# Start-up queues, later loads and a residual by transfer in a fused cosine attention and low-rank mixer

## The chip, the core and the metric

The kernel runs on one core of a Trainium2 chip. The metric is the time of one execution on the device, in microseconds: 582.26 us before the change, the median of three runs (582.1 to 582.92). The profile is of one execution whose span, from the first to the last instruction, is 580.3 us. The engines are named as in the profile: PE multiplies matrices (PEld is its load of the stationary operand), DVE and ACT are the vector and scalar engines, POOL is GpSimd, and SP only issues transfers. SP, ACT and POOL each issue transfers in the order of their own program.

## The reference

Attention over 8 batches of 12 heads, 448 positions and 64 features, with normalised q and k, and then a mixer on the joined heads (768 channels):

```python
q_n = q / (np.linalg.norm(q, axis=-1, keepdims=True) + 1e-06)
k_n = k / (np.linalg.norm(k, axis=-1, keepdims=True) + 1e-06)
scores = np.matmul(q_n, k_n.transpose(0, 1, 3, 2)) / tau
attn = softmax(scores)
x = np.matmul(attn, v)                    # joined to (8, 448, 768)
u = x + (x.transpose(0, 2, 1) @ U @ V).transpose(0, 2, 1)   # rank 32
out = u + np.maximum(u @ w_ch1, 0.0) @ w_ch2                # 768 -> 3072 -> 768
```

The last line adds `u` itself, the residual, to the result of the two large products.

## The kernel before

Two heads make a pair. There are 48 pairs, numbered 0 to 47, six per batch, and the program goes through them in order. For each pair it transposes q and k (T), forms scores by key chunk (S), takes their exponential on ACT, multiplies by v (V), divides, and applies the low-rank product in three steps (A, then a transpose of the divided result X, then H), which leaves `u` transposed, in the tiles `uE` for even and `uO` for odd batches. The two large products of a batch, called M1 (`steps_m1`, L513) and M2 (`steps_m2`, L540), are cut into steps of six matmuls and put between the pairs of the following batch, as filling work for PE.

Inputs come in groups of pairs: groups 0 and 1 hold one pair each, all others two. So group 5 is pairs 8 and 9, group 6 pairs 10 and 11, group 7 pairs 12 and 13. `load` (L205 to L214) brings q, k or v of a group; q takes two transfers, k and v four. Class `Prep` then squares q and k, reduces, takes the root (ACT), inverts (DVE), scales (mostly POOL, L268) and copies v to bf16 (`values`, POOL, L276). Three staging buffers per input are used in turn.

Up to pair 6 the order of everything is written out by hand, in the string `ORDER`. Its words are: `sq0k.a` square k of group 0 on ACT, `red` reduce, `root`, `inv`, `sc` scale, `l3q` load q of group 3, `w62` issue 62 spare matmuls of the identity (L667), which do no work of the result but keep PE busy, `T0`, `Te0` transpose a pair and evict it, `S00` scores of pair 0, chunk 0, `ex00` its exponential, and so on. The identity `ident` is made by POOL and is needed by these spare matmuls and by the transposes of PE.

After that, `put(n, i, fn)` hangs a piece of work behind slot i of pair n, where pair NP is 6; `spread` runs the slots and shares M1 and M2 steps between them. The change and the reasoning touch these entries: the list `at` (squares of q and k, values, two reduces, root) and `when` (inverse and scales) of groups 5, 6 and 7, and the places of their loads. A class `Estimate` counts expected times and only decides which of ACT and DVE evicts a tile.

From pair 12 on, q and k (and X) are transposed by a transfer that SP issues (L315, L461) instead of by PE. For batches after the first, the residual is taken from `ut`: `turn` (L500) transposes half of `u` with one transfer, and DVE adds it as it evicts an M2 block (L558). For batch 0 the residual is instead added by three more matmuls with the identity at the end of each M2 block (L550), and ACT or DVE copies the block out (L554, L556). A half is 384 of the 768 output columns; an M2 block is 24 matmuls of 128x384. Each block is stored by two transfers on SP (L564, L568; for the last blocks of the last batch the second one is ACT's).

The weights `w1_sb` and `w2_sb` are loaded by eight transfers of POOL (L168, L173), from 20.9 us on. `load_mixer` (L137) clears some constants and loads U and V of the mixer on POOL's queue; `load_copies` (L159) loads three more copies of V, which `place_copies` spreads for the later pairs. `V_raw` and `ut` share a tag of two buffers.

## Time and profile before

| engine | busy us | share | instructions |
|---|---|---|---|
| PE | 568.6 | 98% | 5074 |
| DVE | 213.1 | 37% | 461 |
| ACT | 261.0 | 45% | 447 |
| POOL | 215.1 | 37% | 205 |

| group of PE instructions | count | busy us |
|---|---|---|
| L540, M2, 128x384 | 1344 | 233.6 |
| L513, M1, 128x448 | 1128 | 227.2 |
| L331, scores | 576 | 42.4 |
| L667, spare | 144 | 11.1 |
| L550, residual of batch 0 | 18 | 2.0 |

Times of a group are sums over its instructions, which overlap in PE's pipeline; the step from one start to the next is shorter than a mean duration. Six matmuls of M2 take 0.97 to 0.98 us in the chain of waits, so one takes 0.163 us, though the page gives it 327 ns. In the timeline a line gives the start, the length of a merged run, the engine, the line of the kernel and the operation, and in brackets how long the engine sat idle just before and what released it. The transfers moved 74.5 MB, 128 GB/s over the span and 223 to 240 GB/s from 30 to 80 us.

### The profile page before, as it was taken

To read this page: it belongs to the slowest core of one execution; us is meant where nothing else is said; L and a number is where in the kernel's file an instruction comes from. 1 tells how busy PE (TensorE), PEld (TensorE's weight loads), DVE (VectorE), ACT (ScalarE), POOL (GpSimd) and SP (SyncE) were. 2 spreads that over 40 slices of the span, in tenths; PEclk is the share of its full clock that TensorE was granted. 3 is DMA by queue.
4 is the path that set the end of the run, shared out by engine and by line. 5 is a ranking of instruction groups with operands and counts; after the bars stand their busy time and mean duration, and the time that the engine had idled before them with its cause. 6 is when DMAs were issued, how large, how long until landed. Compare 5 with 4: busy or idle time off the path is not lost.

```text
span 580.3 us, 12249 instructions
## 1 busy us (share of the span) xinstructions
PE 568.6 (98%) x5074; PEld 327.1 (56%) x5074; DVE 213.1 (37%) x461; ACT 261.0 (45%) x447; POOL 215.1 (37%) x205
## 2 busy tenths in 40 slices
PE   7999999999999999999999999999999999999997
PEld 6665565555565556555655555655555545655554
DVE  6874551433243334423324343432244332320011
ACT  5876544455333653446324455246443374214200
POOL 8754866515326236426055063253261420000000
PEclk9999999999999999999999999999999999999999
DMA  6999999767486375584465763783655640231022
GB/s 163 193 244 236 238 211 221 181 124 138 103 158 155 88 154 114 135 162 105 88 160 137 128 137 96 145 175 81 134 125 117 132 74 16 54 72 35 7 49 56
DMA packets 139673, 74.52 MB, mean 128 GB/s; under 512 B 86656, under 2 KB 139440, under 8 KB 139616
## 3 DMA queue, kind: packets, MB, share of 16 engines
q1 hardware_dynamic: 129344, 63.03, 50.0%
q0 software_dynamic: 9728, 10.18, 10.3%
q8 instruction: 40, 0.66, 0.4%
q10 hardware_dynamic: 544, 0.51, 0.3%
q14 instruction: 17, 0.14, 0.1%
HBM read 52.19 MB, written 11.01 MB: 109 GB/s over the span
## 4 chain that ended last, share of the span: by engine, by line
PE 87%; DMA 7%; DVE 2%; SPq 1%; ACT 1%; POOL 1%; issue 0%; DVEq 0%; POOLq 0%; ACTq 0%
PE mp L540 38%; PE mp L513 33%; DMA w_sb<-in_moe_w_ch_dram 5%; PE sc L331 5%; PE av L383 3%; PE up L383 2%; DMA kst<-in_k_dram 2%; PE av L343 1%; PE av L376 1%; PE up L376 1%; PE up L469 1%; DMA qst<-in_q_dram 1%; PE av L483 1%; DVE ss L248 1%; ACT E L356 0%
## 5 line engine op out<-in xcount | busy, mean ns | idle before, releaser
L540 PE MATMUL mp<-w_sb,relu 128*128 128x384 bf16 x1344 | 233.6, 327 | 0.8 <-DMA w_sb<-in_moe_w_ch_dram 0.8
L540 PEld LDWEIGHTS <-relu 128*128 128x128 bf16 x1344 | 125.2, 98 | 90.6 <-issue 14.0
L513 PEld LDWEIGHTS <-w_sb 128*128 128x128 bf16 x1128 | 105.0, 98 | 99.2 <-issue 9.3
L517 ACT ACTIVATE relu<-mp 128x448 bf16<-128x448 f32 x162 | 88.0, 543 | 128.4 <-PE mp L513 128.4
L356 ACT ACTIVATE E<-sc 128x896 bf16<-128x896 f32 x144 | 125.2, 923 | 23.6 <-PE sc L331 22.6
L268 POOL TENSOR_TENSOR qk<-kst,inv 128x512 bf16<-128x512 f32 x43 | 45.9, 1069 | 240.7 <-DVE inv L262 236.2
L513 PE MATMUL mp<-uO,w_sb 128*128 128x448 bf16 x576 | 114.3, 353 | 0.0
L513 PE MATMUL mp<-uE,w_sb 128*128 128x448 bf16 x552 | 112.9, 353 | 0.0
L558 DVE TENSOR_TENSOR o_sb<-mp,ut 128x384 f32<-128x384 f32 x50 | 27.8, 557 | 141.4 <-PE mp L540 140.1
L248 DVE TENSOR_REDUCE ss<-sq 128x16 f32<-128x1024 f32 (+1 forms) x50 | 57.8, 1165 | 1.0 <-ACT sq L240 1.0
L268 POOL TENSOR_TENSOR qk<-qst,inv 128x512 bf16<-128x512 f32 x44 | 47.3, 1077 | 1.6 <-PE up L441 1.6
L383 PEld LDWEIGHTS <-E 128*128 128x128 bf16 x1152 | 45.0, 97 | 0.0
L519 DVE TENSOR_SCALAR relu<-mp 128x448 bf16<-128x448 f32 x26 | 16.2, 625 | 78.0 <-PE mp L513 77.5
L331 PE MATMUL sc<-qkT 64*64 64x448 bf16 x576 | 42.4, 360 | 0.6 <-ACT E L356 0.3
L243 POOL TENSOR_TENSOR sq<-kst 128x1024 f32<-128x1024 f32 (+1 forms) x23 | 42.6, 1856 | 0.1
L243 POOL TENSOR_TENSOR sq<-qst 128x1024 f32<-128x1024 f32 x21 | 39.7, 1892 | 3.3 <-DMA qst<-in_q_dram 3.3
L353 ACT ACTIVATE E<-av 128x448 bf16<-128x448 f32 x17 | 9.2, 541 | 47.3 <-PE up L343 47.3
L276 POOL CAST v<-vst 128x1024 bf16<-128x1024 f32 (+1 forms) x25 | 25.0, 1003 | 9.9 <-DMA vst<-in_v_dram 7.7
L383 PE MATMUL av<-v,E 128*128 128x65 bf16 x624 | 28.0, 193 | 0.0
L473 ACT CAST A_sb<-up 128x128 bf16<-128x128 f32 x19 | 5.0, 263 | 47.6 <-PE up L469 47.6
L394 DVE RECIPROCAL rd<-av 128x4 f32<-128x4 f32 x52 | 9.3, 178 | 46.2 <-PE av L383 46.2
L376 PEld LDWEIGHTS <-E 128*128 128x128 bf16 x192 | 18.0, 98 | 14.6 <-issue 0.8
(98 smaller groups left out, 348.9 us busy)
## 6 DMA issues: line engine op xcount, KB each, us to landing
out_dram<-o_sb SPq DMA_DIRECT2D x109, 96.0 KB, 2.2
w_sb<-in_moe_w_ch_dram POOLq DMA_DIRECT2D x8, 1152.0 KB, 18.8
qst<-in_q_dram SPq DMA_DIRECT2D x23, 256.0 KB, 3.9
vst<-in_v_dram SPq DMA_DIRECT2D x46, 128.0 KB, 2.9
kst<-in_k_dram SPq DMA_DIRECT2D x44, 128.0 KB, 2.8
qst<-in_q_dram SPq DMA_DIRECT2D x23, 192.0 KB, 4.0
vst<-in_v_dram SPq DMA_DIRECT2D x46, 96.0 KB, 2.7
kst<-in_k_dram SPq DMA_DIRECT2D x44, 96.0 KB, 2.7
```

The costliest lines, as they stand in the source:

```text
L243: nc.gpsimd.tensor_mul(sq[:, 0:self.nh * 4, :], self.flat(t), self.flat(t))
L248: nc.vector.reduce_sum(self.ss[:, j, 0:self.nh * 4], self.sq[j][:, 0:self.nh * 4, :], axis=AX.X)
L268: eng.tensor_mul(qks[self.gi % 2][:, j, i, :, :, :], t[:, 2 * j:2 * j + 2, :, :].rearrange("p h c d -> p c h d"), iv.unsqueeze(3).to_broad ...
L276: nc.gpsimd.tensor_copy(out=self.flat(v65[self.s])[:, :, 0:D], in_=self.flat(vst[self.s]))
L331: nc.tensor.matmul(out=sc[o:o + 64, h, 0:S], lhsT=t[r, 1, c * 128 + o:c * 128 + o + 64], rhs=t[r, 0, 0:S], start=True, stop=True)
L356: nc.scalar.activation(out=e[:, 2 * c:2 * c + 2, 0:S], in_=sc[:, :, 0:S], func=AF.Exp)
L376: nc.tensor.matmul(out=av[:, i, :, :], lhsT=last_of(b, p)[:, ic * 128:(ic + 1) * 128], rhs=vv[:, 2 * j:2 * j + 2, 3, :], start=(i == 0), s ...
L383: nc.tensor.matmul(out=av[:, i, h, :], lhsT=e[:, 2 * c + h, ic * 128:(ic + 1) * 128], rhs=vv[:, 2 * j + h, c, :], start=False, stop=(i == ...
L513: nc.tensor.matmul(out=mp, lhsT=w1_sb[:, cc, f * 128:(f + 1) * 128], rhs=u[:, cc, 0:S], start=(cc == 0), stop=(cc == CC - 1))
L517: nc.scalar.activation(out=relu[:, f, o:o + S], in_=mp, func=AF.Relu)
L540: nc.tensor.matmul(out=mp, lhsT=relu[:, f, r0:r0 + 128], rhs=w2_sb[:, f, half * HC:(half + 1) * HC], start=(f == 0), stop=(b > 0 and f == ...
L558: nc.vector.tensor_add(o.rearrange("p (k d) -> p k d", d=128), mp.rearrange("p (k d) -> p k d", d=128), ut_of[(b, half)][:, :, c, :])
```

## The change

It has four parts, each with consequences for the order of its queue.

1. The first q is issued by POOL, as the first thing it does, and no longer by SP and ACT. The identity comes after it, and the clearing of constants after that (`pads`), some of it later still (`late_pads`, word `pd`). U and V of the mixer are loaded by ACT behind the first root (word `lm`). `ORDER` exchanges the squares of group 1 (`sq1k.p sq1q.a`) and reduces k before q.
2. The reduces, root and scales of group 5, and the reduces and later steps of group 7, are put earlier; values of group 6 are put later, and its v load too in the order of the program; the v load of group 7 goes behind the first output, and the copies of V go to SP, ahead of the q and k of group 7.
3. The second half of batch 0 takes its residual from a transfer (`turn(0, 1)`), as later batches do, so nine matmuls of L550 go; the first half keeps its nine.
4. The last M2 block is computed, added and stored in two parts, of 256 and 128 columns.

Apart from the nine matmuls and the last block, PE's instructions and their order stay as they were. On SP, `turn(0, 1)` and then the v of group 7 now stand between the first output of batch 0 and the q and k of group 8; the transposes of pairs 12 and 13 come behind these and the second output.

The diff, cut to its core:

```diff
-    make_identity(nc, ident)
-    for t in v65:
-        nc.gpsimd.memset(t[:, :, :, D:D + 1], 1.0)
...
+    def pads():
...
+        nc.gpsimd.memset(U_sb, 0.0)
+        nc.gpsimd.memset(U_raw[64:128, 3, :], 0.0)
...
+    def late_pads():
+        for t in E + E3:
+            nc.gpsimd.memset(t[:, :, S:512], 1.0)
+        nc.gpsimd.memset(V_sb, 0.0)
+
+    def load_mixer():
+        nc.scalar.dma_start(out=U_raw[0:64, :, :], in_=moe_U[0:256].rearrange("(p c) r -> p c r", c=4))
+        nc.scalar.dma_start(out=U_raw[64:128, 0:3, :], in_=moe_U[256:448].rearrange("(p c) r -> p c r", c=3))
+        nc.scalar.dma_start(out=V_raw[0:R, :], in_=moe_V)
...
-            nc.gpsimd.dma_start(out=V_raw[r0:r0 + R, :], in_=moe_V)
+            nc.sync.dma_start(out=V_raw[r0:r0 + R, :], in_=moe_V)
...
-                                 start=(f == 0), stop=(b > 0 and f == NC - 1), skip_group_check=True)
+                                 start=(f == 0), stop=((b, half) != (0, 0) and f == NC - 1),
+                                 skip_group_check=True)
...
-            if b == 0:
+            if (b, half) == (0, 0):
...
+                if (b, half, ci) == (B - 1, 1, len(chunks) - 1):
+
+                    for cs in ((0, 256), (256, 384)):
+                        for i in range(2):
+                            steps.append(lambda half=half, ci=ci, i=i, cs=cs:
+                                         part(half, ci, 12 * i, 12 * i + 12, *cs))
+                    continue
...
+    load(0, "q", nc.gpsimd)
     load(0, "k", nc.sync, nc.scalar)
-    load(0, "q", nc.sync, nc.scalar)
+    make_identity(nc, ident)
...
-    load_mixer()
+    pads()
...
-        sq0k.a red0k sq0q.a red0q root0 inv0 sc0q.v sc0k.v l3q l3k l2v w62 T0 sq1q.a sq1k.p w11
-        Te0 red1q S00 sq2k.p S01 ex00 red1k w8 root1 S02 w26 sq2q.a inv1 red2k sc1k.p ex01 sc1q.p
+        sq0k.a red0k sq0q.a red0q root0 lm inv0 sc0q.v sc0k.v l3q l3k l2v w62 T0 sq1k.p sq1q.a w11
+        Te0 red1k S00 sq2k.p S01 ex00 pd red1q w8 root1 S02 w26 sq2q.a inv1 red2k sc1k.p ex01 sc1q.p
...
         if m == NP + 2:
-            at = [(NP, 1), (NP, 2), (NP + 1, 6), (NP, 5), (NP + 1, 0), (NP + 1, 1)]
-            when = (NP + 1, 2)
+            at = [(NP, 1), (NP, 2), (NP + 1, 6), (NP, 3), (NP, 5), (NP, 6)]
+            when = (NP + 1, 0)
         elif m == NP + 4:
-            at = [(NP + 2, 0), (NP + 2, 1), (NP + 2, 6), (NP + 2, 4), (NP + 2, 6), (NP + 2, 7)]
+            at = [(NP + 2, 0), (NP + 2, 1), (NP + 4, 0), (NP + 2, 4), (NP + 2, 6), (NP + 2, 7)]
             when = (NP + 3, 0)
         elif m == 2 * NP:
-            at = [(m - 3, 6), (m - 3, 6), (m - 1, 0)] + [(m - 2, i) for i in (0, 1, 2)]
-            when = (m - 2, 3)
+            at = [(m - 3, 6), (m - 3, 6), (m - 1, 0), (m - 3, 6)] + [(m - 2, i) for i in (0, 1)]
+            when = (m - 2, 2)
...
-            put(*((NP, 3), (NP + 3, 0))[gi - 6], lambda gi=gi: load_all(gi))
+            at = (((NP, 3), (NP, 3), (NP + 2, 0)), ((NP + 3, 0), (NP + 3, 0), (NP + 4, 4)))[gi - 6]
+            for x, w in zip("qkv", at):
+                put(*w, lambda gi=gi, x=x: load(gi, x, nc.sync))
...
-    put(NP + 3, 0, load_copies)
+    put(NP + 2, 2, load_copies)
+    put(NP + 4, 3, lambda: turn(0, 1))
```

## The prediction

> **What bounds the kernel now.** I read the shares of busy time first, then the slices by window, the waits, and the timeline around each gap of PE.
>
> ```profile
> PE 568.6 (98%) x5074; PEld 327.1 (56%) x5074; DVE 213.1 (37%) x461; ACT 261.0 (45%) x447; POOL 215.1 (37%) x205
> ```
> ```profile
> 0.00:10.00 10.00, 6.72 (x81) 6.26 (x81) 6.51 (x23) 3.21 (x6) 8.94 (x33) 1.00 0.63 177
> 10.00:20.00 10.00, 8.09 (x121) 5.75 (x120) 8.43 (x17) 8.82 (x15) 8.69 (x9) 1.00 0.69 170
> ...
> 80.00:90.00 10.00, 9.05 (x98) 5.62 (x98) 5.58 (x12) 4.42 (x8) 5.43 (x5) 1.00 1.30 214
> 90.00:100.00 10.00, 10.00 (x98) 5.97 (x97) 1.83 (x5) 4.14 (x7) 6.45 (x8) 1.00 1.13 226
> ```
>
> The first page line shows PE at 98%. The windows (length, busy PE, PEld, DVE, ACT, POOL, clock, DMA share, GB/s) show where the rest is: PE is short of 10 only before 90 us, and part of its early work is spare matmuls (L667). From 90 to 569 us PE is full, so only fewer PE instructions help there. Idle time of other engines counts for nothing.
>
> The start and its four visible gaps, from the timeline (start, length, engine, line, operation):
>
> ```profile
> 1.37 5.37 PE L667 MATMUL mp<-ident 128*128 128x128 bf16 x62 [1.37 <-POOL ident masks.py:199]
> ...
> 5.06 0.63 ACT L240 ACTIVATE sq<-qst 128x512 f32<-128x512 f32 x1 [0.47 <-DMA qst<-in_q_dram]
> ...
> 8.45 0.40 PE L300 MATMUL tp<-ident,qk 128*128 128x128 bf16 x4 [1.71 <-DVE qk L268]
> ...
> 9.85 0.63 ACT L240 ACTIVATE sq<-qst 128x512 f32<-128x512 f32 x1 [2.85 <-DMA qst<-in_q_dram]
> ```
> ```profile
> 60.36 0.40 PE L300 MATMUL tp<-ident,qk 128*128 128x128 bf16 x4 [0.46 <-POOL qk L268]
> ...
> 80.46 1.14 PE L540 MATMUL mp<-w_sb,relu 128*128 128x384 bf16 x6 [0.82 <-DMA w_sb<-in_moe_w_ch_dram]
> ...
> 87.60 0.38 PE L416 MATMUL av<-X,U_sb 128*128 128x128 bf16 x4 [0.49 <-DVE X L395]
> ```
>
> The first two squares wait for the first and second q to land; 60.36, 80.46 and 87.60 are stalls of PE itself: 0.46 + 0.82 + 0.49 = 1.77 us.
>
> **What the Trainium skill says.** "DMA: Bandwidth & Descriptors", section Latency and other measured facts, puts the first byte of a GpSimd transfer at about 1 us against 0.6 for SP and ACT. The trace agrees in sign: k of 128 KB from GpSimd's queue lands 3.3 us after issue, from SP 2.8. The same page, SWDGE vs HWDGE vs iDMA, says that both kinds end on the same 16 DMA engines, taken in turn, so every load delays the weights; the DMA share of 1.13 to 1.30 up to 100 us agrees. "SBUF — State Buffer", section SBUF: two separate sides, warns that a VectorE two-port operation keeps GpSimd from writing descriptors. VectorE does only memsets of 0.17 to 0.27 us until 4.4 us; I expect no such block, but no row shows GpSimd issuing at 0.7 us.
>
> **The change part by part.**
>
> First q. GpSimd is free at 0.74. Its first k rows took 0.77 and 0.60 to issue and 3.3 and 3.0 to land, at the same 128 and 96 KB. So q lands near 0.74 + 3.3 = 4.0 and 1.51 + 3.0 = 4.5, against 5.06 now. ACT squares k until 4.60, then q: 0.46 earlier at best. Both bounds: nothing gained if q takes bandwidth from k, which ends ACT's wait at 3.97; 0.85 lost if q needs 4.4 us, as V_raw did on this queue (1.51 + 4.4 = 5.9). I take 0.45 less a little. SP has one q issue less (0.65 + 0.05), so the second q lands 9.1, not 9.76, which serves the chain sq, reduce, root that follows. ident comes 2 x about 0.69 = 1.37 later, so 62 spare matmuls end at 6.74 + 1.37 = 8.11. The first transpose would then want PE at 8.0: 0.1 on its first half, hidden since the k half waits for DVE until 8.6. GpSimd: 2.7 after ident, k issues 2.6, pads 2.4, so its square starts at 7.7 and both end at 10.65 (2.89 us now). late_pads, four memsets of 1.1 and V_sb 0.5, end at 12.25; the inverse that GpSimd awaits ends at 12.87 - 0.5 = 12.37. Just hidden. ACT's three mixer issues (1.8 us) lie in its 2.85 us wait before 9.85. The start thus gives 0.45 (0.85 lost to 0.65). It survives to 90 us only if weights follow: the third w1 piece was issued at 41.64 and landed 12.9 later, at 54.5, and PE begins its part at 54.93, a slack of 0.4.
>
> Earlier reductions of pairs 8 and 9. Their inverse came at 58.1, GpSimd's four scales (1.05 each) ran 58.23 to 62.3. Both squares are done at 49.07. With reduces right after it and root behind the second exp (52.1 to 53.8), the scales start near 55 and end near 59, before the transpose at 59.5: -0.46.
>
> Values of pairs 12 and 13. Their loads (SP, 65.74 to 70.9) ran ahead of need against the w2 piece that landed at 50.89 + 29.52 = 80.41. They now stand behind the first output, past 84 us: 448 KB less. V copies move forward: 168 KB more. (448 - 168) KB at 223 GB/s is 1.3 us. PE arrives earlier too, by 0.45 + 0.46, so of 0.82 about 0.6 goes (0.2 to 0.82).
>
> Stall at 87.60. DVE had two reduces (1.2 each) and an output copy between the halves of pair 9; reduces come earlier, the copy goes to ACT: -0.35 (0 to 0.49).
>
> Residual by transfer. Nine matmuls of 128x128 go. Each group of three starts 0.17 before the next instruction (83.20 to 83.37): -0.5. DVE adds of 0.557 replace copies of about 0.5, hidden: DVE is busy 1.83 of 10 us from 90 to 100. The transfer lands 3.9 us after issue, at about 90, and its first reader is at 101.8: hidden.
>
> But SP is a queue. Between these lines it had been waiting for outputs:
>
> ```profile
> 84.16 0.54 SPq L564 DMA_DIRECT2D out_dram<-o_sb  x1
> ...
> 91.64 0.52 SPq L564 DMA_DIRECT2D out_dram<-o_sb  x1
> 92.20 0.60 SPq L568 DMA_DIRECT2D out_dram<-o_sb  x1
> 92.90 4.35 SPq L315 DMA_TRANSPOSE qkT<-qk  x2
> ```
>
> In PE's old time scale the queue now has, from 84.4 (the copy is ACT's and 0.2 later): outputs 1.25, ut transfer 1.6, values 2.8, q and k of the next group 4.0, outputs 1.25, total 10.9, so the transposes of pair 12 start at 95.3, not 92.9. They landed 4.9 to 5.4 after issue here (median 4.0 over the kernel). PE's scores of pair 12 start at 98.83 without a wait now. New stall: 95.3 + 4.0 - 98.83 = 0.5 to 95.3 + 5.4 - 98.83 = 1.9; shorter if the queue packs tighter. I take 0.8, as the weights' traffic ends sooner. Behind it, X's transposes have about 1 us of slack.
>
> Last block in two parts.
>
> ```profile
> 576.22 0.56 DVE L558 TENSOR_TENSOR o_sb<-mp,ut 128x384 f32<-128x384 f32 x1 [3.34 <-PE mp L540]
> ```
>
> A third of its columns remain at the end: the add falls from 0.56 to about 0.29 (taking one 0.16 us base and 1.04 ns per column), and the last output is 32 KB, not 96, so it lands slightly sooner. PE issues 24 matmuls more, but 256 plus 128 columns at the 0.425 ns per column of 0.163 us for 384 is the same sum plus perhaps 0.1. Net -0.3 (0 to -0.6).
>
> Sum: -0.45 - 0.46 - 0.6 - 0.35 + 0.8 - 0.5 - 0.3 = -1.86; 582.26 - 1.86 = 580.4.
>
> **The rivals.**
> 1. The SP queue holds: pair 12 is transposed in time. For it: median landing 4.0, DMA less loaded. Against it: 4.9 to 5.4 in this place. -1.86 - 0.8 = -2.66: 579.6.
> 2. The ramp is bound by transfers anyway: the earlier start is taken back by w1 (slack 0.4) and the stall of pair 12 is 1.6. For it: DMA share over 1 from 30 to 100 us. -1.86 + 0.4 + 0.8 = -0.66: 581.6.
> 3. Slower: first q by GpSimd's queue comes late. For it: V_raw's 4.4 us, GpSimd's first descriptors of the run. Instead of 0.45 gained, 0.85 lost (+1.3), the w2 gain doesn't show (+0.6), pair 12 waits 1.6 (+0.8), and X's transposes come 0.5 late: -1.86 + 3.2 = +1.3: 583.6. Against it: k's 3.3 and 3.0 on the same queue.
>
> **How the numbers follow.** 0.5 for my forecast (580.4), 0.2 for rival 1, 0.18 for rival 2, 0.12 for rival 3. Faster by over 0.2% is below 581.1: forecast and rival 1, 0.70. Rival 2 is within 0.2%: 0.18. Rival 3 is slower: 0.12. The range leaves out the outer part of rival 1 (below 579.0) and rival 3: 579.0 to 582.4.
>
> **What would show it.** The second square of ACT at about 4.6 and the third at 9.2; no wait at the transpose of 60.36, one under 0.3 us at the M2 step of 80.46; nine fewer L550 matmuls; a wait of PE for the transfer of qkT before the scores of pair 12, 0.3 to 1.5 us; an end add of about 0.3. Wrong if q lands after 5.1, if PE waits for weights near 54 us, or if SP starts pair 12's transposes early enough.

## The result, and the profile after

The changed kernel takes 587.26 us (586.51 to 588.52, six runs), and the kernel before 582.4 us (582.1 to 583.46, six runs) beside it: a ratio of 1.0082, with a 95% interval of 1.0067 to 1.0097. The change makes the kernel about 4.8 us slower. The prediction of 580.4 us was wrong, and its range, up to 582.4, did not hold the time.

In the profile after, most line numbers stand 2 to 6 higher: scores are L333, transposes L302, M1 L515, M2 L542, squares L242 (ACT) and L245 (POOL), scales L270, the two output transfers L567 and L571, spare matmuls L673, transposes by transfer L317, `turn` L502.

The first line of the page, and the slices by window (length, busy PE, PEld, DVE, ACT, POOL, granted clock of PE, DMA share, GB/s):

```profile
PE 570.1 (97%) x5089; PEld 329.5 (56%) x5089; DVE 213.9 (37%) x462; ACT 260.7 (45%) x447; POOL 213.9 (37%) x201
```
```profile
0.00:10.00 10.00, 5.97 (x66) 5.80 (x66) 6.41 (x22) 3.36 (x6) 8.39 (x28) 1.00 0.72 184
10.00:20.00 10.00, 8.47 (x130) 6.28 (x131) 8.22 (x15) 7.64 (x14) 8.94 (x12) 1.00 0.61 150
80.00:90.00 10.00, 10.00 (x112) 6.16 (x110) 5.51 (x11) 5.49 (x10) 6.33 (x6) 1.00 1.30 211
90.00:100.00 10.00, 7.46 (x72) 4.69 (x68) 1.21 (x4) 2.82 (x5) 2.64 (x5) 1.00 1.18 208
100.00:110.00 10.00, 7.92 (x62) 4.60 (x63) 3.15 (x7) 2.27 (x3) 4.20 (x3) 0.66 0.81 177
```

From 80 to 90 us PE is now full, where it was 9.05. But from 90 to 110 us it is idle for 4.6 us, and in the second of these windows its clock is 0.66. Before, both windows were full at a clock of 1.00; the second of them was:

```profile
100.00:110.00 10.00, 10.00 (x107) 5.92 (x106) 5.14 (x11) 5.39 (x11) 2.46 (x3) 1.00 0.72 162
```

The three stalls are gone. In the timeline the same three steps carry no bracket any more:

```profile
60.34 0.61 PE L302 MATMUL tp<-ident,qk 128*128 128x128 bf16 x8
...
79.66 1.14 PE L542 MATMUL mp<-w_sb,relu 128*128 128x384 bf16 x6
...
86.15 0.39 PE L418 MATMUL av<-X,U_sb 128*128 128x128 bf16 x4
```

The start is later, not earlier. The timeline of the first 11 us, where the engines stand under each other:

```profile
1.28 0.77 POOL L207 DMA_DIRECT2D qst<-in_q_dram  x1 [0.84 <-POOLq L905]
...
4.97 0.63 ACT L242 ACTIVATE sq<-kst 128x512 f32<-128x512 f32 x1 [2.94 <-DMA kst<-in_k_dram]
5.50 0.61 ACT L242 ACTIVATE sq<-qst 128x512 f32<-128x512 f32 x1
...
8.29 3.63 POOL L245 TENSOR_TENSOR sq<-kst 128x512 f32<-128x512 f32 x2
...
8.64 1.53 DVE L270 TENSOR_TENSOR qk<-kst,inv 128x512 bf16<-128x512 f32 x1
...
10.22 0.40 PE L302 MATMUL tp<-ident,qk 128*128 128x128 bf16 x4 [0.95 <-DVE qk L270]
```

In the kernel before, the square and the scale of k stood so:

```profile
3.97 0.63 ACT L240 ACTIVATE sq<-kst 128x512 f32<-128x512 f32 x1 [1.94 <-DMA kst<-in_k_dram]
...
8.31 0.69 DVE L268 TENSOR_TENSOR qk<-kst,inv 128x512 bf16<-128x512 f32 x1
```

The first q is issued at 1.28, not 0.74. Its second transfer is issued at 2.05 and takes 3.1 us to land, so q is there near 5.15, no sooner than before, when ACT began its square at 5.06. And k, whose issue times are unchanged, lands 1.0 later: its square begins at 4.97 in place of 3.97. The scale of k then starts 0.33 later and takes 1.53 us where it took 0.69, which is 0.84 more. Together the second half of the first transpose comes 1.17 later than before (9.05), and of this 0.82 is left at the first A V of pair 0 (16.46, was 15.64).

The loss lies at the scores of pair 12. SP's queue, with start and length of each issue, and then PE:

```profile
83.48 0.54 SPq L567 DMA_DIRECT2D out_dram<-o_sb  x1
84.06 0.60 SPq L571 DMA_DIRECT2D out_dram<-o_sb  x1
84.70 3.39 SPq L502 DMA_TRANSPOSE ut<-uE  x1
88.21 0.69 SPq L213 DMA_DIRECT2D vst<-in_v_dram  x1
...
94.31 1.54 SPq L215 DMA_DIRECT2D kst<-in_k_dram  x1
...
97.19 0.59 SPq L571 DMA_DIRECT2D out_dram<-o_sb  x1
98.43 2.67 SPq L317 DMA_TRANSPOSE qkT<-qk  x2
```
```profile
102.08 0.96 PE L333 MATMUL sc<-qkT 64*64 64x448 bf16 x8 [4.63 <-DMA qkT<-qk]
102.98 2.10 PE L542 MATMUL mp<-w_sb,relu 128*128 128x384 bf16 x6
```

Before, the same scores started without a wait:

```profile
98.83 0.57 PE L331 MATMUL sc<-qkT 64*64 64x448 bf16 x8
```

The turn's single issue holds SP for 3.39 us, and what follows is late as well: the two transposes by transfer, of pairs 12 and 13, are issued from 98.43 on in place of 92.90. PE waits 4.63 us for them. Then six M2 matmuls take 2.10 us, where they take 1.14 elsewhere: the clock has fallen. Between 82 and 100 us two of SP's waits are put down to earlier transfers that had to land:

```profile
SPq L214 <- DMA ut<-uE: 0.7, 1, 0.7
...
SPq L317 <- DMA qst<-in_q_dram: 0.5, 1, 0.5
```

The transposes of pair 12 (L317) waited 0.5 us for the landing of q of pairs 14 and 15, which they don't read.

The end, where one 128x384 addition of 0.56 us stood:

```profile
579.87 0.42 DVE L561 TENSOR_TENSOR o_sb<-mp,ut 128x256 f32<-128x256 f32 x1 [2.06 <-PE mp L542]
581.21 0.29 DVE L561 TENSOR_TENSOR o_sb<-mp,ut 128x128 f32<-128x128 f32 x1 [0.92 <-PE mp L542]
```

A ledger from the two timelines, after less before, each from the start times of the same instruction:

| stretch | us |
|---|---|
| start, to the A V of pair 0 (16.46 less 15.64) | +0.82 |
| to the M2 step ahead of pair 12's scores (95.34 less 96.78, so -1.44 in all) | -2.26 |
| to pair 12's scores (102.08 less 98.83, so +3.25 in all) | +4.69 |
| to the first M1 step of batch 1 (117.35 less 112.41, so +4.94 in all) | +1.69 |
| to the end of the span (584.7 less 580.3, so +4.4 in all) | -0.54 |

Each trace is one execution. Four runs below have the same program as the changed kernel up to 84 us; in their traces the A V of pair 0 starts between 16.46 and 16.67 us, and PE's wait for the weights w2 near 80 us is 0, 0.19, 0.43 and 0.66 us. So the first line of the ledger is good to some 0.3 us (two traces of the start of the kernel before have 15.64 and 15.36), and the second, which counts this wait as gone, to some 0.7.

### The profile page after: what moved, and what is told of

Read it like the earlier page. It is cut to its first block, busy times and chain, and to the rows that moved or that the text cites. A ratio compares the mean times of both kernels' runs of the same rounds, so it can differ in the third digit from the quotient of the medians.

```text
span 584.7 us, 12288 instructions
## 1 busy us (share of the span) xinstructions
PE 570.1 (97%) x5089; PEld 329.5 (56%) x5089; DVE 213.9 (37%) x462; ACT 260.7 (45%) x447; POOL 213.9 (37%) x201
## 4 chain that ended last, share of the span: by engine, by line
PE 92%; DMA 2%; DVE 2%; ACT 1%; SPq 1%; issue 1%; POOL 1%; POOLq 0%; DVEq 0%
PE mp L515 37%; PE mp L542 36%; PE sc L333 6%; PE av L385 3%; PE up L385 2%; DMA vst<-in_v_dram 1%; PE av L378 1%; PE av L345 1%; PE tp L302 1%; PE sc L659 1%; PE up L378 1%; PE up L471 1%; DMA qst<-in_q_dram 1%; DMA qkT<-qk 1%; PE av L485 1%
## 5 line engine op out<-in xcount | busy, mean ns | idle before, releaser
L542 PE MATMUL mp<-w_sb,relu 128*128 128x384 bf16 (+2 forms) x1368 | 234.9, 325 | 0.0
L542 PEld LDWEIGHTS <-relu 128*128 128x128 bf16 x1368 | 127.2, 98 | 89.6 <-issue 14.6
L515 PEld LDWEIGHTS <-w_sb 128*128 128x128 bf16 x1128 | 105.1, 98 | 99.3 <-issue 9.7
L270 POOL TENSOR_TENSOR qk<-kst,inv 128x512 bf16<-128x512 f32 x43 | 45.9, 1068 | 243.4 <-DVE inv L264 235.5
L515 PE MATMUL mp<-uO,w_sb 128*128 128x448 bf16 x576 | 114.2, 352 | 0.0
L515 PE MATMUL mp<-uE,w_sb 128*128 128x448 bf16 x552 | 112.9, 353 | 0.0
L561 DVE TENSOR_TENSOR o_sb<-mp,ut 128x384 f32<-128x384 f32 (+2 forms) x54 | 29.7, 550 | 144.7 <-PE mp L542 142.6
L270 POOL TENSOR_TENSOR qk<-qst,inv 128x512 bf16<-128x512 f32 x44 | 47.3, 1077 | 2.2 <-PE up L443 2.2
L333 PE MATMUL sc<-qkT 64*64 64x448 bf16 x576 | 42.7, 362 | 5.2 <-DMA qkT<-qk 4.6
L245 POOL TENSOR_TENSOR sq<-kst 128x1024 f32<-128x1024 f32 (+1 forms) x23 | 43.4, 1887 | 0.0
L245 POOL TENSOR_TENSOR sq<-qst 128x1024 f32<-128x1024 f32 x21 | 39.7, 1892 | 3.0 <-DMA qst<-in_q_dram 3.0
L385 PE MATMUL av<-v,E 128*128 128x65 bf16 x624 | 28.3, 194 | 0.0
```

What stands on the lines that cost most here:

```text
L245: nc.gpsimd.tensor_mul(sq[:, 0:self.nh * 4, :], self.flat(t), self.flat(t))
L270: eng.tensor_mul(qks[self.gi % 2][:, j, i, :, :, :], t[:, 2 * j:2 * j + 2, :, :].rearrange("p h c d -> p c h d"), iv.unsqueeze(3).to_broad ...
L333: nc.tensor.matmul(out=sc[o:o + 64, h, 0:S], lhsT=t[r, 1, c * 128 + o:c * 128 + o + 64], rhs=t[r, 0, 0:S], start=True, stop=True)
L385: nc.tensor.matmul(out=av[:, i, h, :], lhsT=e[:, 2 * c + h, ic * 128:(ic + 1) * 128], rhs=vv[:, 2 * j + h, c, :], start=False, stop=(i == ...
L515: nc.tensor.matmul(out=mp, lhsT=w1_sb[:, cc, f * 128:(f + 1) * 128], rhs=u[:, cc, 0:S], start=(cc == 0), stop=(cc == CC - 1))
L542: nc.tensor.matmul(out=mp, lhsT=relu[:, f, r0:r0 + 128], rhs=w2_sb[:, f, half * HC + c0:half * HC + c1], start=(f == 0), stop=((b, half) ! ...
```

## The experiments

Three ideas were set against each other. QUEUE: the order and number of issues on SP make pair 12's transposes late. TRANSFER: the turn's own transfer is slow and slows others while the weights are still coming in, wherever it stands. START: the new start-up alone makes the kernel slow. Later CLOCK was added: part of the loss is PE's lower clock after the pause. Times of the kernel before were 581.91, 582.13, 581.96, 582.58 and 582.13 us beside the five groups of runs, so the ratios are what is compared.

### The residual by matmuls again

```diff
-                                 start=(f == 0), stop=((b, half) != (0, 0) and f == NC - 1),
+                                 start=(f == 0), stop=(b > 0 and f == NC - 1),
...
-            if (b, half) == (0, 0):
+            if b == 0:
...
-    put(NP + 4, 3, lambda: turn(0, 1))
```

> The changed kernel, with the second half of batch 0 taking its residual from nine matmuls again (no ut transfer of batch 0). Theory QUEUE (pair 12's transposes come late because the ut issue of 3.39 us and the values of pairs 12 and 13, 2.8 us, stand ahead of them on SP): they start about 3.4 us earlier, near 95; PE waits about 1 us for them instead of 4.63, too short for its clock to fall (2.2 us more), and the nine matmuls cost 0.5: about 582 us. Rival START (the loss is the start-up, 0.8 us and what follows): the wait at pair 12 stays above 3 us, 585 to 587 us.

Measured: 582.07 us, ratio 0.9997 (0.9982 to 1.0012). SP's queue and PE:

```profile
94.90 2.77 SPq L317 DMA_TRANSPOSE qkT<-qk  x2
...
98.35 0.57 PE L333 MATMUL sc<-qkT 64*64 64x448 bf16 x8 [0.74 <-DMA qkT<-qk]
```

Without the turn the transposes are issued 3.5 us earlier, PE waits 0.74 in place of 4.63 us and keeps its clock. M1 of batch 1 starts at 111.94 in place of 117.35. So the one edit that was to save nine matmuls costs some 5 us, and it makes the whole of the slowdown. Whether by the queue or by the transfer this run can't say.

### The values of pairs 12 and 13 loaded where they were

```diff
-            at = (((NP, 3), (NP, 3), (NP + 2, 0)), ((NP + 3, 0), (NP + 3, 0), (NP + 4, 4)))[gi - 6]
+            at = (((NP, 3), (NP, 3), (NP + 2, 0)), ((NP + 3, 0), (NP + 3, 0), (NP + 3, 0)))[gi - 6]
```

> The changed kernel, with the v load of pairs 12 and 13 put back where it was, ahead of the first output on SP. QUEUE: transposes of pair 12 start 2.8 us earlier, wait 1.5 to 2 us, no fall of the clock; up to 0.8 us of the wait for w2 near 80 us comes back: about 583 us. Rival TRANSFER (the ut transfer itself, 8.9 us to land under load, holds everything behind it): wait above 3 us and the clock falls: 586 us or more.

Measured: 586.72 us, ratio 1.0079 (1.0055 to 1.0104). The wait for w2 is back (1.19 us at 81.29). The four issues of v, 2.7 us, are gone from behind the turn, but the transposes are issued at 97.00, only 1.4 earlier; the turn took 3.68 us to issue and 9.1 to land. PE still waits 2.99 us and gets pair 12's data at 102.08, as in the changed kernel: the transfer takes 5.0 us to land where it took 3.65, and the wait is shorter only because PE itself comes 1.64 later. Counting issues is not enough: QUEUE alone fails here.

### The turn ahead of the first output

```diff
-    put(NP + 4, 3, lambda: turn(0, 1))
+    put(NP + 3, 0, lambda: turn(0, 1))
```

> The changed kernel, with the ut transfer of batch 0 issued while SP is idle (behind the q and k of pairs 12 and 13, near 68 us) instead of behind the first output. QUEUE: as with the residual by matmuls, wait about 1 us, and the nine matmuls stay saved: about 581.5 us. Rival TRANSFER: the transfer loads the engines as much there and delays w2, so a wait of about a microsecond appears near 80 us: about 582.5 us.

Measured: 584.64 us, ratio 1.0051 (1.0036 to 1.0066). SP has nothing to do at that place, and yet, on SP and then on PE:

```profile
69.01 6.65 SPq L502 DMA_TRANSPOSE ut<-uE  x1
...
83.28 2.08 PE L542 MATMUL mp<-w_sb,relu 128*128 128x384 bf16 x6 [3.23 <-DMA w_sb<-in_moe_w_ch_dram]
```

Now the turn takes 6.65 us to issue and 16.3 to land, and the second piece of w2 lands at 83.2 in place of 79.3. Of these 3.9 us, 2.9 come after its issue (31.2 us to land in place of 28.3); the rest is a later issue, before the turn. The wait for pair 12 is gone, and a wait of 3.23 us for weights has come, also with half clock behind it (0.50 from 84 to 88 us). At both places tried, while the weights come in, the turn costs three to five microseconds by the ratios (1.0051 and 1.0082 against 0.9997 without it). This speaks for TRANSFER.

### The old start-up in the changed kernel

The first q by SP and ACT, `ident`, the constants and ORDER's first two lines as in the kernel before; nothing else.

```diff
-    load(0, "q", nc.gpsimd)
     load(0, "k", nc.sync, nc.scalar)
-    make_identity(nc, ident)
+    load(0, "q", nc.sync, nc.scalar)
...
-    pads()
+    load_mixer()
```

> The changed kernel with the old start-up (first q by SP and ACT, all constants cleared first, U and V by GpSimd, old order of the squares), all else changed. QUEUE: only the 0.82 us comes back that the first values step of PE shows (16.46 against 15.64): 586.4 us, with the wait at pair 12 still above 4 us. Rival START: below 584 us.

Measured: 586.22 us, ratio 1.0076 (1.0061 to 1.0091). The A V of pair 0 comes 1.0 earlier, and PE then waits 4.87 us for pair 12's transposes, issued at 97.67. The start is not what makes the kernel slow. On SP the turn's own issue is short here, and the one behind it is held up instead:

```profile
83.67 1.62 SPq L500 DMA_TRANSPOSE ut<-uE  x1
85.40 2.35 SPq L211 DMA_DIRECT2D vst<-in_v_dram  x1
```

Together the two hold SP for 4.1 us, against 4.2 in the changed kernel; the turn takes 9.1 us to land.

### Spare matmuls in the pause, 60 and 110

```diff
+        if n == 2 * NP:
+            warm = psum.tile([128, 512], FP, name="mp", tag="ps_m", bufs=2)
+            for _ in range(60):
+                nc.tensor.matmul(out=warm[:, 0:128], lhsT=ident, rhs=ident, start=True, stop=True)
```
```diff
-            for _ in range(60):
+            for _ in range(110):
```

> The changed kernel with 60 spare 128x128 matmuls (ident by ident, their output unused) put on TensorE ahead of the scores of pair 12, where it stands idle for 4.63 us in the changed kernel. Nothing else differs. CLOCK (the pause costs twice: 4.63 us of waiting, and then about 2.2 us because TensorE runs at half its clock for some 5 us after it): 60 matmuls of some 0.055 us fill 3.3 us of the pause, the scores of pair 12 still start near 102.1, but at the full clock, so that the first block of M1 of batch 1 starts at 115.1 in place of 117.35, and the time is 585.0. If the slow stretch after the pause has another cause (for one, operands that arrive late), the half clock stays, M1 starts at 117.3 and the time is 587.3.

> The changed kernel with 110 spare matmuls (ident by ident, their output unused) ahead of the scores of pair 12, in place of 60, so that TensorE works through the whole of the wait. CLOCK: 110 by 0.055 us end near 103.5, after the transposes have landed, so that TensorE has no pause above 0.3 us there; the granted clock stays at 1.0 from 98 to 112, and the first M1 of batch 1 comes 13.1 to 13.3 us after the scores of pair 12, the distance without a clock fall (98.35 to 111.94 less the 0.5 of nine matmuls), where it was 15.27 in the changed kernel and 14.71 with 60 spare matmuls. If the slow stretch comes from something other than the pause, the distance stays near 15 and the clock falls to 0.5 all the same. Time: 586.5 with the clock kept, 588.7 without.

Measured: with 60, 585.85 us, ratio 1.0057 (1.0041 to 1.0073); with 110, 586.89 us, 1.0079 (1.0066 to 1.0093). The windows of the changed kernel, of the one with 60 and of the one with 110, columns as above:

```profile
98.00:100.00 2.00, 0.00 (x0) 0.00 (x0) 0.00 (x0) 0.00 (x0) 2.00 (x5) 0.98 1.09 243
100.00:102.00 2.00, 0.00 (x0) 0.00 (x0) 0.00 (x0) 0.00 (x0) 2.00 (x2) 0.50 1.31 186
102.00:104.00 2.00, 1.92 (x12) 0.71 (x13) 0.00 (x0) 1.28 (x2) 1.16 (x1) 0.50 0.65 165
104.00:106.00 2.00, 2.00 (x19) 1.40 (x18) 0.00 (x1) 0.45 (x1) 0.00 (x0) 0.50 0.72 180
106.00:108.00 2.00, 2.00 (x22) 1.31 (x21) 1.18 (x4) 0.00 (x0) 1.04 (x1) 0.81 0.44 104
```
```profile
104.00:106.00 2.00, 2.00 (x14) 1.14 (x13) 0.00 (x0) 1.32 (x2) 0.09 (x1) 0.50 0.63 168
106.00:108.00 2.00, 2.00 (x23) 1.33 (x21) 0.66 (x3) 0.00 (x0) 0.12 (x1) 0.70 0.48 112
```
```profile
104.00:106.00 2.00, 2.00 (x25) 1.15 (x23) 0.00 (x0) 1.17 (x2) 0.36 (x1) 1.00 0.41 94
106.00:108.00 2.00, 2.00 (x36) 1.56 (x34) 1.05 (x3) 0.56 (x1) 0.00 (x0) 1.00 0.69 181
```

With 60, a pause of 1.86 us was left, and in the profiled run the clock still fell to 0.50 for 3.4 us. That run is the slowest of its four; the other three have a mean clock of 0.999 or 1.000, so there it hardly fell, and their 585.00 to 585.95 us are near the 585.0 expected with a kept clock. With 110 there is no pause and no fall; the time gains nothing, because the spare matmuls put off the scores themselves, to 104.39 from 102.08. From pair 12's scores to M1 of batch 1 it is 15.27 us in the changed kernel, 14.71 with 60 and 13.08 with 110 (117.47 less 104.39). So CLOCK holds: with the pause filled the clock stays, and 15.27 less 13.08, that is 2.2 us of the loss, is the clock's. It also gives the nine matmuls their price: 13.58 us before less 13.08 is 0.50.

### q and k of pairs 14 and 15 behind the transposes

```diff
-            at = {2 * NP + 2: [(m - 4, 5), (m - 4, 6), (m - 3, 2)],
+            at = {2 * NP + 2: [(m - 3, 2), (m - 3, 2), (m - 3, 2)],
```

> The changed kernel with the loads of q and k of pairs 14 and 15 issued behind the transposing transfers of pairs 12 and 13 on SyncE's queue, in place of ahead of them; the early turn of u for the residual stays. QUEUE (what is ahead of pair 12's transposes on SyncE's queue makes them late: the backlog behind the turn, and the q and k of pairs 14 and 15 whose slots wait for landings): the transposes are issued by 92.5 (the v's last issue at 90.9 and two output issues of 0.6 each) and land within 3.5 to 5.5 us, by 98; TensorE waits under 0.5 us for them and keeps its clock; M1 of batch 1 starts near 110.6 (117.35 less 4.63 and 2.2) and the time is 580.4, a ratio of 0.997. TRANSFER (the bytes of the turn keep the transfers behind until the last weights have landed, at 92.4): the transposes issued at 92.5 take 7 us or more to land, TensorE still waits 1.5 to 2.5 us at the scores of pair 12 and the time is 582.5 to 584.5. In both, the later squares of pairs 14 and 15 could make a new wait near their scores; it would show as a wait for a scale by VectorE or GpSimd near 125 us.

> As the run before it (q and k of pairs 14 and 15 behind the transposes of pairs 12 and 13), and with the start-up of the kernel before (both halves of the first q on SyncE's and ScalarE's queues, the identity first on GpSimd, the constants ahead of the loop). START: the first matmuls of the transposes, the scores and the A V all come 0.8 to 1.0 us earlier than in that run, and where no wait for a transfer stands after them the whole of it reaches the end: 579.5 if the run before it gives 580.4, and in any case 0.8 to 1.0 less than that run. QUEUE and TRANSFER as above. If the start's loss were swallowed by the wait for w2 or for pair 12, the difference would be under 0.3.

Measured: 583.85 us, ratio 1.0030 (1.0010 to 1.0051), and with the old start-up 582.8 us, 1.0012 (0.9995 to 1.0028). The first of the two, SP and PE:

```profile
93.73 4.83 SPq L317 DMA_TRANSPOSE qkT<-qk  x2
...
99.67 0.57 PE L333 MATMUL sc<-qkT 64*64 64x448 bf16 x8 [1.11 <-DMA qkT<-qk]
...
114.96 0.35 PE L515 MATMUL mp<-uO,w_sb 128*128 128x448 bf16 x1 [1.09 <-DVE uO L490]
```

The transposes are issued 4.7 us earlier than in the changed kernel, but PE gets pair 12's data only 2.4 us earlier (99.67, was 102.08): from issue to landing that transfer now takes 5.9 us in place of 3.65. So the queue ahead of the transposes cost about half of the wait. The other half is not gone: the landing is 2.3 us longer, and PE sees only 1.11 of it because it comes to this place 1.11 us later itself (98.56, was 97.45; 0.66 of it is a wait for w2). Both theories hold in part. Expected under QUEUE was no wait over 0.5, under TRANSFER 1.5 to 2.5; it is 1.11.

At 114.96 and 116.53 there are two new waits of 1.09 and 1.22 us: the loads moved behind pair 12 push the transposing transfer of X to 111.45, and DVE, which waits for it for 3.73 us, is late with the block that M1 needs and then with an addition. What one issue gained in this queue, another lost. Behind these two pauses the clock falls again, although neither is long:

```profile
116.00:118.00 2.00, 1.47 (x6) 0.62 (x6) 0.48 (x2) 0.00 (x0) 0.47 (x1) 0.74 0.63 177
118.00:120.00 2.00, 2.00 (x19) 1.33 (x18) 0.51 (x2) 0.54 (x1) 1.43 (x1) 0.50 0.66 166
```

Five of the twelve executions have a mean clock of 0.997 or less, and so have the seven slowest of the twenty with the old start-up (584.58 us and more); the profiled ones are among them. The old start-up brings 1.05 us here by the medians, about what was expected, though the two intervals overlap.

### The new start-up alone, and its parts

The kernel before with the changed start-up (as in the diff above, without the later edits); then that with q on SP and ACT again and `ident` first:

```diff
-    load(0, "q", nc.gpsimd)
-    load(0, "k", nc.sync, nc.scalar)
     make_identity(nc, ident)
+    load(0, "k", nc.sync, nc.scalar)
+    load(0, "q", nc.sync, nc.scalar)
```

and then the start-up alone with the word `pd` ahead of the square of k:

```diff
-        sq0k.a red0k sq0q.a red0q root0 lm inv0 sc0q.v sc0k.v l3q l3k l2v w62 T0 sq1k.p sq1q.a w11
-        Te0 red1k S00 sq2k.p S01 ex00 pd red1q w8 root1 S02 w26 sq2q.a inv1 red2k sc1k.p ex01 sc1q.p
+        sq0k.a red0k sq0q.a red0q root0 lm inv0 sc0q.v sc0k.v l3q l3k l2v w62 T0 pd sq1k.p sq1q.a w11
+        Te0 red1k S00 sq2k.p S01 ex00 red1q w8 root1 S02 w26 sq2q.a inv1 red2k sc1k.p ex01 sc1q.p
```

> The kernel before with the new start-up alone: first q by GpSimd's queue ahead of the identity, the memsets in two groups, mixer loads by ScalarE, and GpSimd's square of k of group 1 ahead of ScalarE's of q. No turn, no moved loads, no tail. START (the new start-up costs what the changed kernel's trace shows, 0.82 us at the A V of pair 0): first scores at 11.4 (10.24 in the kernel before), A V at 16.46, and of the 0.8 us some part is swallowed where TensorE waits for w1 and w2 (60.36, 80.46) and for the transposes (87.60): the end is 0.3 to 0.8 us later, a time of 582.6 to 583.0. If the predicted gain of the start (0.45) were only hidden by the other edits, it would be 581.7.

> As the run before it (the kernel before with the new start-up alone), but the first q goes by SyncE's and ScalarE's queues behind k, as in the kernel before, and the identity is first on GpSimd again. It tells the two causes of the late start apart. SHARING (q by a third queue takes bandwidth from k, which then lands 1.0 us later): k's square starts at 3.97 again, the root near 6.45, the scale of q at 7.70. OVERLAP (GpSimd's square runs at the time of VectorE's scale of k, and this takes 1.5 in place of 0.69 us): it stays, if GpSimd is done with its memsets by 8.3; the second scale ends near 9.8 and the first scores start near 11.1, 0.3 before the run before it. If both were one cause, the scale would take 0.69 and the scores start at 10.2.

> As the start-up alone, but GpSimd does the late group of memsets (of E and V, about 1.5 us) ahead of its square of k of group 1, not after it, so that it doesn't square while VectorE scales k. OVERLAP: the scale of k takes 0.69 us again, the first scores start at 10.6 (11.4 less 0.84), while k still lands late (square at 4.97). The square of k of group 1 then starts near 9.8 and its scale of pair 1 comes later, which costs nothing as long as T of pair 1 does not wait. Time 0.5 to 0.8 less than with the start-up alone. If the long scale comes from something else (the load of DMA writes at that time), it stays at 1.5 us and the scores at 11.4.

Measured: start-up alone 582.89 us, ratio 1.0013 (0.9999 to 1.0026); q by SP 585.44 us, 1.0067 (1.0044 to 1.0091); memsets first 583.13 us, 1.0017 (1.0005 to 1.0028).

Alone, the start-up puts T of pair 6 (60.36 before) at 61.69, 1.33 late, and M1 of batch 1 at 112.98, only 0.57 late: the wait for w2 at 80.46, 0.82 us, is no longer there. The late start is partly paid out of that wait. The interval of the ratio takes in 1, so the time alone does not show a loss.

With the memsets first (timeline of DVE, POOL and PE):

```profile
8.74 0.69 DVE L270 TENSOR_TENSOR qk<-kst,inv 128x512 bf16<-128x512 f32 x1
...
9.63 2.90 POOL L245 TENSOR_TENSOR sq<-kst 128x512 f32<-128x512 f32 x2
...
10.67 0.57 PE L333 MATMUL sc<-qkT 64*64 64x448 bf16 x8 [0.17 <-DVE qkT L307]
...
80.82 1.14 PE L542 MATMUL mp<-w_sb,relu 128*128 128x384 bf16 x6 [0.98 <-DMA w_sb<-in_moe_w_ch_dram]
```

POOL squares after DVE's scale, and the scale takes 0.69 us again: this shows that the overlap is the cause of the 1.53. The scores start 0.8 earlier, as expected. But the time is no better, against an expected 0.5 to 0.8: the wait for w2 is back, with 0.98 us. A change of the start is worth little here as long as w2 lands when it does.

With q by SP and ACT the expectation was badly missed: k is squared at 4.61 (3.97 was expected, 4.98 is the start-up alone), but q only at 6.83 (5.06 in the kernel before), and DVE's scale of q takes 2.05 us beside POOL's square. In this kernel POOL, free of memsets, issues k of group 2 at 1.46, not 3.51, ahead of the q's at 2.01 and 2.27. That k is squared only after 9 us, and it shares the transfers of the first 5 us. SP's and ACT's issues up to 2.7 us stand where they stood in the kernel before. So the run fits SHARING, in that a load from a third queue makes those beside it land later, and it suggests that the memsets at the head of the kernel before had a use: they held that load back. It is no proof: the load was not moved alone.

There is a further cost in this run. PE has nothing to do until the late q is scaled:

```profile
11.80 1.21 PE L302 MATMUL tp<-ident,qk 128*128 128x128 bf16 x8 [4.26 <-DVE qk L270]
```

Behind this pause its clock is 0.50 from 10.1 to 17.0 us, and the mean clock is 0.991 to 0.994 in all seven executions. How much of the 3.5 us of this run is the clock's and how much the late q's was not separated.

### What is left without the turn and the start-up

The changed kernel with both undone (the edits of the first and of the old start-up's diff together); then, on the kernel before, the last block in two parts alone, and the moved loads, reductions and scales alone:

```diff
+                if (b, half, ci) == (B - 1, 1, len(chunks) - 1):
+                    for cs in ((0, 256), (256, 384)):
...
+                    continue
```
```diff
-            at = [(NP, 1), (NP, 2), (NP + 1, 6), (NP, 5), (NP + 1, 0), (NP + 1, 1)]
-            when = (NP + 1, 2)
+            at = [(NP, 1), (NP, 2), (NP + 1, 6), (NP, 3), (NP, 5), (NP, 6)]
+            when = (NP + 1, 0)
...
-            put(*((NP, 3), (NP + 3, 0))[gi - 6], lambda gi=gi: load_all(gi))
+            at = (((NP, 3), (NP, 3), (NP + 2, 0)), ((NP + 3, 0), (NP + 3, 0), (NP + 4, 4)))[gi - 6]
...
-    put(NP + 3, 0, load_copies)
+    put(NP + 2, 2, load_copies)
```

> The changed kernel with the start-up of the kernel before and with the residual of half 1 of batch 0 by nine matmuls again (no early turn): what is left is the moved loads of pairs 10 to 13, the copies of V by SyncE and the last block in two parts. By the ledger: the turn's run with matmuls stood at 582.07 against 581.91 for the kernel before, with M1 of batch 1 at 111.94 (112.41 before) in spite of a start 0.82 later. Without the late start: M1 at 111.1 to 111.4, and with the tail 0.4 earlier the end comes 1.2 to 1.6 us before that of the kernel before: 580.3 to 580.8, a ratio of 0.9975. If the start's loss is swallowed by the wait at pair 12's scores (0.74 us there), it is 581.7.

> The kernel before with the last block of the output in two parts alone, 256 and then 128 columns wide. Nothing differs before the last 5 us. As the prediction had it: the last matmul comes 0.1 later (48 matmuls in place of 24), the eviction of the last part takes 0.29 in place of 0.56 us and its transfer is a third as large, so the last store ends 0.3 to 0.5 us earlier: a time of 581.6, a ratio of 0.9992. If the tail is hidden or costs as much as it brings, the ratio is 1.000; with an interval of about 0.001, the time alone hardly tells these apart, so the span from M1 of batch 1 to the end is read too: 467.9 us in the kernel before, 467.4 expected here.

> The kernel before with the moved loads alone: the values of pairs 10 and 11 and of pairs 12 and 13 later, the reductions, roots and scales of pairs 8 to 13 moved as in the change, the copies of V by SyncE and earlier. Old start-up, nine residual matmuls, old tail. If the moves bring what the prediction had for 60.36, 80.46 and 87.60 less what the first scores of pair 12 then wait (0.6 to 0.7 us in the two runs with these moves and no turn), TensorE's pauses from 37 to 112 us fall from 1.77 to 1.0 us, M1 of batch 1 starts 96.0 us after the A V of pair 0 (96.8 in the kernel before), and the time is 581.2 to 581.5. If the gain of the run with the old start and no turn was the tail's alone, it is 582.0 or above.

Measured: both undone 580.86 us, ratio 0.9977 (0.9968 to 0.9986), which beats both kernels; the tail alone 581.19 us, 0.9974 (0.9963 to 0.9985); the moves alone 581.25 us, 0.9983 (0.9972 to 0.9995). The end of the tail alone, and pair 12 in the moves alone:

```profile
575.36 0.29 DVE L559 TENSOR_TENSOR o_sb<-mp,ut 128x128 f32<-128x128 f32 x1 [0.91 <-PE mp L540]
```
```profile
97.69 0.57 PE L331 MATMUL sc<-qkT 64*64 64x448 bf16 x8 [0.96 <-DMA qkT<-qk]
```

With the tail alone, from M1 of batch 1 to the end it is 467.2 us (578.7 less 111.50), 0.7 less than before (467.9): 0.2 by the additions and 0.5 by the last store, which takes 3.05 in place of 3.52 us from the last addition to the end. The measured gain, 0.0026 or 1.5 us, is larger. In its trace M1 of batch 1 starts 0.9 earlier, with a wait for w2 of 0.18 in place of 0.82, though both programs are the same up to the last block. A spread of this size stands between other traces of one program, as said under the ledger. And the kernel before took 582.58 us beside this group, 0.45 to 0.67 more than beside the other four. So about half of that ratio can't be put down to the edit.

With the moves alone PE has one pause from 37 to 112 us, the 0.96 above, where there were three of 1.77. M1 of batch 1 starts at 111.27, 1.1 earlier than before. So they bring about what their steps gave them. The gains of tail and moves don't add up in the sum of both (0.0023 against 0.0026 and 0.0017); the intervals are too wide to say more.

## Why the prediction was wrong, by its own steps

Right, with the sizes:

- **60.36, 80.46 and 87.60.** Predicted -0.46, -0.6 and -0.35; all three pauses went in the profiled execution. Read from the start times around each they gave -0.63, -0.99 and -0.64, the -2.26 of the ledger, each 0.15 to 0.17 more than the idle in its bracket. The bracket counts from the end of the last matmul, and without a pause the next one starts before that end. The -0.99 is of one execution; with the waits of 0 to 0.66 us in the four others of the same program, the mean gain at w2 is near the -0.6 predicted.
- **Nine matmuls.** Predicted -0.5; 0.50 by the distance without a clock fall.
- **The last block.** Predicted -0.3; -0.54 in the ledger, -0.7 alone. It was mis-sized at the last store.
- **The weights follow.** w1 made no wait near 54 us, and the start's change went through to 60 us.

Wrong, the second of these most of all, with 4.63 us of waiting where 0.8 was forecast:

- **First q: -0.45 became +0.82.** Three things failed. POOL was taken to be free at 0.74 and issued first at 1.28; with 3.1 us to land (3.0 was assumed for this transfer) q was there near 5.15 and not at 4.5, so there was nothing to gain. The prediction's own sign of being wrong, a landing after 5.1, came. Second, the sentence that bounded the case "nothing gained if q takes bandwidth from k" at zero: k landed 1.0 us later, and a later k costs: with the later q it puts DVE's scale of k back by 0.33. The bound had to be negative. Third, the step took POOL's squares from their old place (9.38) to the time of DVE's scale without asking what the two do to each other; that alone is 0.84 on the scale. The Trainium skill, "SBUF — State Buffer", section Who interferes with whom, says that a VectorE instruction with two SBUF inputs contends with a GpSimd instruction that reads SBUF. The trace agrees: 0.69 and 2.89 us apart, 1.53 and 3.63 together; and 2.05 for the scale of q where POOL had started first. The prediction read another sentence of that page, on memsets and descriptors, and not this one.
- **SP's queue: the transposes of pair 12 at 95.3, a wait of 0.8 us; measured 98.43 and 4.63.** The sum of 10.9 us was right in kind and its terms were issue lengths of an unloaded queue. Measured, from 83.48: outputs 1.2, turn 3.5, values 2.8, q and k 5.6, outputs 1.2, and a wait of 0.65, in all 14.95, which is 4.05 more; the first output was 0.92 earlier than taken, hence 98.43 and not 99.35. So the turn was mis-sized by 1.9 (1.6 is what later turns take, after the weights are in), q and k by 1.6, where single issues were held up for as long as 1.54, and the wait ahead of the transposes was left out. The landing was not what failed: 98.43 to 102.08 is 3.65, less than the 4.0 to 5.4 assumed. PE wanted the data at 97.45 (102.08 less 4.63), 1.38 before the old 98.83, so the gain of the three stalls was there and was spent in this wait. The step also took PE and SP to move forward together; PE came 1.38 earlier and SP's first output only 0.92, since the stall at 87.60 lies behind that output. With these terms the forecast becomes the measurement: 0.8, and 4.05 for the queue, and 0.46 for PE, less 0.68 for the landing (3.65 where 0.8 implied 4.33), is 4.63.
- **The transfer itself.** The turn was taken to land in 3.9 us, "hidden". It took 8.9 to 9.5 us and, when issued at 69 us, 16.3. Its landing was hidden, and its share of the transfers was not: in the run with the turn early the second piece of w2 took 2.9 us longer to land.
- **The clock.** No step asked what a wait of PE costs after it ends. It cost 2.2 us. "TensorE: Matmul & The Clock Gate" of the skill, Part 1: The HAM clock gate, says that the clock is halved after an idle window of about 3.4 us and comes back after as long a busy time. The trace agrees in size: clock 0.50 from 99.9 us, 2.5 us into the pause of 4.63, until about 106.8 (0.81 in the window from 106 to 108), that is for 6.8 us. It differs in the threshold: a pause of 1.86 us was also followed by half clock, and so were two of 1.09 and 1.22 us close together. Nor is the length of a pause enough to tell: pauses of 1.71 us (kernel before, at 8.45) to 1.97 us (moves alone, at 8.89) were not followed by it.

With the measured terms: +0.82 - 2.26 + 4.69 + 2.19 - 0.50 - 0.54 = +4.4, the difference of the two spans. Rival 3, the slower one, had the right sign of the start and of the wait at pair 12, but for the wait no more than 1.6 us, and no rival had the clock. The forecast's own sentence, "shorter if the queue packs tighter", had only one side; the queue packed looser.

What stays open: how much of the turn's cost is the time SP is held and how much is the share it takes of the transfers. That the turn is the cause is shown by the run without it; the split is not. The data of pair 12 come 3.73 us earlier without the turn, and 2.41 earlier with the turn but without the q and k of pairs 14 and 15 ahead of them. A turn in two or three smaller transfers, or one after the weights are in, was not tried; in the changed kernel the first addition that reads it starts at 107.43, while w2's last piece lands at 92.4.

## What to carry to other kernels

Price an issue and a landing from rows in the same state of the transfers, not from the median of the kernel: here the turn and the issue behind it held SP for 2.4 us late in the kernel (at 407 us), and for 3.8 to 4.5 us at 85 us, when weights were loading; the turn at 69 us held it for 6.65 us alone. When an edit adds an item to an in-order queue, add up the queue's waits for landings as well as its issue times, and follow everything that stands behind it; and ask of each new pause of PE what a slow clock behind it would cost: here every pause of 2.99 us or more had one, and shorter ones had it or not. When work is brought forward, look at what runs on the other engines at its new time: an earlier q took from k, and earlier squares on POOL took from DVE's scale.

## What the runs showed of the hardware that was not expected

- A transposing transfer from SBUF to SBUF of half of `u`, issued by SP: a median of 1.5 us of issue and about 4 us of landing over the kernel. At 85 us, with weights coming in, 3.39 to 3.69 us of issue with the new start-up; with the old one 1.62 and 1.59, and then 2.35 and 2.14 for the load behind it, which takes about 0.7 us elsewhere. The landings there are 8.9 to 9.5 us. At 69 us it took 6.65 us to issue and 16.3 to land. The two issues for pairs 12 and 13 together took 2.67 to 5.62 us.
- PE's clock was at 0.50 for 6.8 us in five traces in which PE was still waiting when it fell (pauses of 2.99 to 4.87 us), and for 3.4 us in three in which PE was back at work by then (a pause of 1.86 us; pauses of 1.09 and 1.22 us; pauses of 1.04 and 1.28 us). In the 3.4 us before each fall PE had been idle for some 1.9 us or more. The reverse does not hold: at 7 to 10 us some traces have as much idle time and no fall, with pauses of up to 1.97 us.
- POOL's first transfer of the kernel was issued only at 1.28 us, 0.84 idle after its last memset at 0.34; its first memset of the identity, in the kernel before, ran at 0.74.
- DVE's scale beside POOL's square of the same shape: 1.53 or 2.05 us in place of 0.69, in the latter case with POOL's two squares at their full speed (2.89 us).
- Five traces of one program differ by up to 0.66 us in a single wait for weights near 80 us, and by 0.2 us in the first 17 us.
